# The state's matmuls of a chunked attention on all four 64x64 parts of TensorE: later 64 tokens with the heads of a pair swapped, three copies of y

## The chip, the core and the metric

The kernel runs on one core of one Trainium2 chip. The metric is device microseconds for one execution of the whole program; lower is better. Three runs of the kernel before took 645.78 us in the median (644.98 to 647.78).

## The reference, cut to what matters

The program computes a linear attention with a decaying state and, on its output, two feed-forward layers. For each of 4 batch rows and 8 heads, over 768 tokens of 48 features:

```
for t in range(S):
    cur = einsum('bhd,bhe->bhde', u[None] * kt, vt)
    y[:, :, t] = einsum('bhd,bhde->bhe', rt, state + cur)
    state = wt[..., None] * state + einsum('bhd,bhe->bhde', kt, vt)
x = y.transpose(0, 2, 1, 3).reshape(B * S, H * D)     # 3072 tokens x 384
x = max(x @ w1, x @ w2, x @ w3) @ w_out               # 384 -> 768 -> 384
h = x @ w_in                                          # 384 -> 1024
solu = h * softmax(h)                                 # then a layer norm with g_ln, then @ w_out
```

Everything is float32. The large matrix products are done as three products of rounded high and low parts, so that a product of one 128-wide tile is nine matmuls where its depth is 384.

## The kernel before, in words

The 768 tokens are cut into 6 chunks of 128, and a **unit** u is one chunk of one batch row: 24 units, u // 4 is the chunk. A unit's tokens are taken in two halves of 64 (j = 0, 1), and its 8 heads in 4 pairs p of two heads e = 0, 1. A head has 64 rows (48 and padding), so a pair fills the 128 partitions: head e stands on partitions 64e to 64e + 63. All attention matmuls are 64x64 with 64 columns: what they load comes from one half of the partitions, which picks the array's upper or lower 64 rows, and what they write goes to one half of the partitions of PSUM, which picks its left or right 64 columns. So an instruction uses one of four parts of the array, and each float32 instruction appears in the trace as two matmul records.

A unit's chain, by function and line: prefix and suffix products of the decays on VectorE (`s_sfx` L399, `s_pfx` L416), r scaled by them (`s_rp` L420), scores on TensorE (`s_score` L474), a masked copy of the scores over a diagonal (`s_mask` L481), y within the half (`s_intra` L536, rows by token half j, columns by head e), the state's increments (`s_state2` L582), the state at the middle and at the end (`s_mid` L604, `s_end` L610 on VectorE), and then the state's part of y (`s_inter` L548), which adds to the same PSUM tile as `s_intra`. There y's half j lies in bank j, and head e on partitions 64e of both banks. `s_inter` loads the state of head e from partitions 64e and writes to partitions 64e: two of the four parts. ScalarE then copies y out of PSUM (`s_yT` L662), small DMAs move rows (L668), and `s_xt` (L688, L687) splits it into high and low parts, which are the input of the first feed-forward layer.

The feed-forward layers take tiles of 2 or 3 units (units 0-1, 2-3, 4-5, 6-8, 9-11 and so on): 18 groups of nine matmuls in the first (`stage_a`, L737), then the second (`stage_b`, L767). Each group's result leaves PSUM by ScalarE (L742) or VectorE (L744), then is split (L747, L750). While units 7 to 12 run, a later layer's weights are also converted (`middle_weights`, L318 and L323 on VectorE). After the last unit the last weights are converted and the third and fourth products run, 24 times (L1175, L1252).

The order of all instructions up to there is made by a planner in the file (`Plan`): every task has an engine, an estimated duration in ns, a due time and what it reads and writes. The planner runs them through a model of the engines, and each engine then executes its instructions strictly in the order that comes out. So a changed estimate moves instructions on every engine. y has one PSUM tile of two banks, which the copy of one unit frees for the next.

Of the kernel before, what the change touches and what calls it, by code (L numbers as in the profile page):

```python
# [10 lines left out]
AF = mybir.ActivationFunctionType  # L11
# [3 lines left out]
B, H, T, D = 4, 8, 768, 48  # L15
L = 128
HL = L // 2
NC_ = T // L
NU = B * NC_
NP = H // 2  # L20
# [7 lines left out]
DV = 64  # L28
# [13 lines left out]
BOTH, STEP, AHEAD = 41000, 45600, 20000  # L42
C_DUE = (20000, 2200)
SLACK = 1500
CUT = 0.5
GRP = [(0, 0), (0, 0), (0, 0), (1, 1), (1, 1, 1, 2)]
CW = 384
# [37 lines left out]
class Plan:  # L85
# [8 lines left out]
    def add(self, eng, ns, due, fn, reads=(), writes=(), after=(), take=None, give=None, kb=0, port=0, slack=0):  # L94


        t = Task(len(self.tasks), eng, ns, due, fn)
        t.take, t.give, t.load, t.port, t.slack = take, give, kb, port, slack
        for k in reads:
            t.deps.update(self.wrote.get(k, ()))  # L100
        for k in writes:
            t.deps.update(self.wrote.get(k, ()))
            t.deps.update(self.read.get(k, ()))
        t.deps.update(x for x in after if x is not None)
        for k in reads:
            self.read.setdefault(k, []).append(t)
        for k in writes:
            self.wrote[k], self.read[k] = [t], []
        t.deps.discard(t)
        self.tasks.append(t)  # L110
        return t
# [66 lines left out]
def emit(tc, general, flag, fm, tm, ub, wa, win, wo2, g, cst, half_cst, lmask, out):  # L178
    nc = tc.nc
    PS = bass.MemoryType.PSUM  # L180
    V, A, G, PE = nc.vector, nc.scalar, nc.gpsimd, nc.tensor
# [6 lines left out]
    with ExitStack() as top:  # L188
# [25 lines left out]
        def parts(u):  # L214
            p3 = lambda x: x.rearrange("p (a b) -> p a b", a=NP)
            return p3(r_t[u]), p3(kw_t[u][:, 0:NP * L]), kw_t[u][:, NP * L:]
# [33 lines left out]
        def load_v(u, eng=A):  # L250
            if u < NU and u not in v_t:
                v_t[u] = apool.tile([128, H * DV], F32, tag="v", name=f"v{u}")
                eng.dma_start(v_t[u], tm[u][:, 2 * DM:])
# [203 lines left out]
        def pair(tag, name):  # L457

            t = ps_a.tile([128, 2, 512], F32, tag=tag, name=name)
            return t[:, :, 0:NP * HL].rearrange("p j (a b) -> p j a b", a=NP)  # L460
# [22 lines left out]
        def gen_score(u):  # L483
# [39 lines left out]
            V.memset(d1, 0.0)  # L523
            V.memset(d1[:, :, 0:1], 1.0)

        def s_intra(u):
            d = at[u]
            c = u // B
            v = v_t[u]
            d["yp"] = y = pair("y", f"y{u}")  # L530
            for p in range(NP):
                for j in range(2):
                    for e in range(2):
                        h = 2 * p + e
                        o = slice(64 * j, 64 * j + 64)
                        PE.matmul(y[64 * e:64 * e + 64, j, p], v[o, h * DV:(h + 1) * DV], d["a"][o, h],  # L536
                                  start=(p == 0), stop=(c == 0 and j == 0 and p == NP - 1))

        def s_inter(u):

            d = at[u]
            rt = parts(u)[0]
            for j in (1, 0) if u // B else (1,):
                s = d["st1"] if j else d["st"]
                for p in range(NP):
                    for e in range(2):
                        o = slice(64 * e, 64 * e + 64)
                        PE.matmul(d["yp"][o, j, p], s[o, p], rt[o, p, j * HL:(j + 1) * HL],  # L548
                                  start=False, stop=(p == NP - 1))

        def s_y(u):
            d = at[u]
# [103 lines left out]
        def s_yT(u):  # L656
            ps = at[u]["yp"]
            xf[u] = x = apool.tile([128, NP, L], F32, tag="xf", bufs=1 if general else 3, name=f"xf{u}")
            if general:
                A.activation(x, ps, AF.Copy)  # L660
            else:
                A.activation(x.rearrange("p a (j t) -> p j a t", j=2), ps, AF.Copy)  # L662
            if general:
                s_rows(u)

        def s_rows(u):
            for k in range(KX):
                nc.sync.dma_start(xf[u][3::4, k], xf[u][k::4, KX])  # L668
# [118 lines left out]
        st = {}  # L787
# [65 lines left out]
        def general_phase1():  # L853
# [89 lines left out]
            for j in range(2, n_tile):  # L943
# [9 lines left out]
                if j + 2 == n_tile:  # L953
                    cut = int(len(gs) * CUT)
                    run_groups(gs[:cut], pos, k1, run_items=run_items)
# [11 lines left out]
        def fast_phase1():  # L967
# [6 lines left out]
            def due_of(u):  # L974
                j = tile_of[u]
                last = need[j] - AHEAD
                gap = (need[j] - need[j - 1]) / tiles[j] if j > 1 else START[3]
                return last - gap * (first[j] + tiles[j] - 1 - u)

            def attend(u):  # L980
                d = at.setdefault(u, {})
                D_ = due_of(u)
                late_by = SLACK if u >= first[2] else 0
                late = u // B
                r_, k_, w_ = ("r", u % 2), ("k", u if u < 3 else (u - 3) % 2), ("w", u if u < 3 else (u - 3) % 2)
                rk_ = ("rk", 2 if u == 2 else (u if u < 2 else u - 1) % 2)
                v_, a_, s_, x_ = ("v", u % 2), ("a", u in (1, 3)), ("s", u % 2), ("xf", u % 3)
                sb = ("sbd", u % B)
                add = lambda eng, ns, off, fn, *a, **k: P.add(eng, ns, D_ + off, fn, *a, **k)
                add("SP", 400, -9000, lambda: load_part(u, 2), writes=[w_], kb=260)  # L990
                add("SP", 400, -8000, lambda: load_part(u, 1), writes=[k_], kb=256)
                add("SP", 400, -7000, lambda: load_part(u, 0), writes=[r_], kb=256)
                add("SP", 400, -6500, lambda: load_rk(u, nc.sync), writes=[rk_, "rk in order"], kb=384)
                add("SP", 400, -3000, lambda: load_v(u, nc.sync), writes=[v_, "v in order"], kb=256)
                add("DVE", 1620, 0, lambda: s_sfx(u), [w_], ["sf", "d1", ("pts", u)], port=250)
                add("POOL", 1200, 1500, lambda: d["kt"](), ["sf"], [k_])
                add("DVE", 1230, 2500, lambda: s_pfx(u), [w_, "d1"], ["pf"], port=250)
                add("ACT", 830, 9000, lambda: s_stat(u), [], [w_])
                add("DVE", 680, 3500, lambda: s_rp(u), ["pf"], [r_], port=650)
                add("POOL", 1100, 500, lambda: s_rk(u), [], [rk_])  # L1000
                add("DVE", 1150, 3800, lambda: (s_rku(u), s_diag(u)), [rk_, "u"], [s_], port=600)
                add("POOL", 1050, 4500, lambda: s_dg(u), [s_, "cs"], [a_])
                add("PE", 750, 4600, lambda: s_score(u), [r_, k_], ["sc in order"], slack=late_by, take=("s", ("sc", u)))
                sc = P.tasks[-1]
                if u < NPT:
                    add("PE", 950, 4700, lambda: s_kTp(u), [k_, "ident"], take=("m", ("kTp", u)))
                    add("ACT", 580, 4800, lambda: d["kTe"](), [], ["kT"], after=P.tasks[-1:], give=("m", ("kTp", u)))
                else:
                    add("DVE", 700, 4000, lambda: s_kq(u), [k_], ["sf"])
                    add("SP", 330, 4500, lambda: s_kd(u), ["sf"], [("kd", u % 2)], kb=256)  # L1010
                    add("SP", 2500, 5000, lambda: s_kT(u), [("kd", u % 2)], ["kT"], kb=400)
                add("DVE", 720, 5500, lambda: s_mask(u), ["cs"], [a_], after=[sc], give=("s", ("sc", u)))
                add("PE", 750, 6500, lambda: s_intra(u), [a_, v_], [("y", u), "y in order"], slack=late_by, take=("y", ("y", u)))
                add("PE", 750, 6600, lambda: s_state(u), ["kT", v_], ["ds in order"], P.tasks[-1:], take=("s", ("ds", u)))
                ds = P.tasks[-1]
                if late:
                    add("POOL", 620, 3000, lambda: s_decay(u), [sb, ("pts", u)], ["st"])
                add("DVE" if late else "ACT", 430, 7500, lambda: s_mid(u), ["st"] if late else [], ["st1"], after=[ds],
                    give=None if late < NC_ - 1 else ("s", ("ds", u)))
                if late < NC_ - 1:  # L1020
                    add("DVE", 430, 8000, lambda: s_end(u), ["st1"], [sb], after=[ds], give=("s", ("ds", u)))
                add("PE", 950 if late else 600, 8500, lambda: s_inter(u), ["st", "st1", r_], [("y", u)], slack=late_by)
                add("ACT", 580, 9500, lambda: s_yT(u), [("y", u)], [x_], give=("y", ("y", u)))
                add("SP", 1700, 9800, lambda: s_rows(u), [], [x_], kb=48)

            def split(u, after=()):
# [336 lines left out]
```

## Time and profile before

| what | value |
|---|---|
| median of three runs | 645.78 us |
| the profiled execution | 645.44 us, span of its instructions 643.6 us |
| TensorE busy | 600.4 us (93%) |
| VectorE busy | 429.3 us (67%) |
| ScalarE busy | 295.7 us (46%) |
| GpSimd busy | 382.3 us (59%) |
| mean granted TensorE clock | 0.991 |

PE is TensorE, PEld its weight loads, DVE VectorE, ACT ScalarE, POOL GpSimd, SP the queue that issues the DMAs. The time of an execution is its span and some 2 us around it. A chain of waits follows the work that ended last back to what released each step; its first table gives the shares of the span by line. In a timeline, a row is a start, a duration, the engine, the line, and in brackets the idle time before it and what ended it. Matmuls are pipelined, so their durations overlap: how long a group of them holds the engine is read from one group's start to the next one's.

### The profile page before, as it was taken

How to read it: one execution, taken by the hardware profiler on the slowest of the kernel's cores; microseconds unless marked ns; L12 is line 12 of the kernel's file. 1: busy time of each engine (PE TensorE's matmuls, PEld its weight loads, DVE VectorE, ACT ScalarE, POOL GpSimd, SP SyncE). 2: the span in 40 equal slices, each digit the busy share in tenths (PEclk: the TensorE clock that was granted, in tenths of full speed). 3: DMA queues.
4: the chain of work that ended last, by engine and by line, in shares of the span. 5: the costliest groups of instructions: out<-in, count | busy, mean ns of one | idle time of the engine just before them, and what ended most of it. 6: DMA issues, size and time to landing. Idle time of an engine off the chain costs nothing.

```text
span 643.6 us, 15413 instructions
## 1 busy us (share of the span) xinstructions
PE 600.4 (93%) x5926; PEld 556.6 (86%) x5926; DVE 429.3 (67%) x785; ACT 295.7 (46%) x689; POOL 382.3 (59%) x525
## 2 busy tenths in 40 slices
PE   2577999999999999999999989989999999999996
PEld 2466898999999999999999979987899988888895
DVE  6999977689988755665662222538777777777750
ACT  2878853355453232232232125636555555555552
POOL 4888865567667444454353232655977777777762
PEclk9998999999999999999999999999999999999999
DMA  8968454676564454444332103203776666666661
GB/s 308 345 213 274 150 143 128 177 235 200 165 181 113 130 141 118 130 133 127 104 87 70 21 5 108 78 17 98 146 169 146 148 157 150 152 155 156 155 124 57
DMA packets 174340, 91.93 MB, mean 143 GB/s; under 512 B 140976, under 2 KB 148912, under 8 KB 174256
## 3 DMA queue, kind: packets, MB, share of 16 engines
q1 hardware_dynamic: 174256, 90.84, 52.2%
q8 instruction: 49, 0.80, 0.5%
q14 instruction: 35, 0.29, 0.1%
HBM read 67.87 MB, written 21.76 MB: 139 GB/s over the span
## 4 chain that ended last, share of the span: by engine, by line
PE 73%; DVE 5%; DMA 3%; issue 2%; POOL 2%; ACT 2%; SPq 0%; DVEq 0%; ACTq 0%; POOLq 0%
PE a L737 26%; PE o L1252 16%; PE h L1175 14%; PE b L767 10%; PE y L548 3%; PE sc L474 2%; PE y L536 2%; PE ds L582 1%; DMA fr<-in_fm_dram 1%; DVE x L744 1%; POOL h L750 1%; POOL wo L336 1%; DMA kd<-sf 1%; DVE x L318 1%; DVE sf L399 1%
## 5 line engine op out<-in xcount | busy, mean ns | idle before, releaser
L737 PE MATMUL a<-xh,wah 128*128 128x384 f32 (+1 forms) x432 | 145.8, 337 | 5.2 <-DVE x L744 3.1
L737 PE MATMUL a<-xl,wah 128*128 128x384 f32 (+1 forms) x432 | 140.6, 326 | 0.4 <-POOL xl L687 0.4
L737 PE MATMUL a<-xh,wal 128*128 128x384 f32 (+1 forms) x432 | 140.5, 325 | 0.0
L1252 PE MATMUL o<-wo,lh 128*128 128x384 f32 x368 | 94.0, 337 | 0.0
L737 PEld LDWEIGHTS a<-xh,wah 128*128 128x128 f32 x432 | 83.0, 192 | 9.4 <-DVE x L744 4.4
L1175 PE MATMUL h<-wi,x2h 128*128 128x512 f32 x288 | 90.6, 396 | 0.0
L750 POOL TENSOR_TENSOR h<-x,h 128x384 fp32r<-128x384 f32 (+1 forms) x48 | 51.1, 1065 | 62.3 <-ACT h L747 62.2
L744 DVE TENSOR_TENSOR x<-a,x 128x384 f32<-128x384 f32 (+1 forms) x108 | 54.4, 505 | 46.3 <-PE a L737 35.5
L737 PEld LDWEIGHTS a<-xl,wah 128*128 128x128 f32 x432 | 83.1, 192 | 0.7 <-POOL xl L687 0.7
L737 PEld LDWEIGHTS a<-xh,wal 128*128 128x128 f32 x432 | 83.1, 192 | 0.0
L1244 POOL TENSOR_TENSOR ll<-c,lh 128x512 fp32r<-128x512 f32 x44 | 64.6, 1490 | 21.6 <-ACT lh L1243 21.5
L767 PE MATMUL b<-h,wbh 128*128 128x384 f32 (+1 forms) x288 | 70.9, 332 | 0.0
L1252 PEld LDWEIGHTS o<-wo,lh 128*128 128x128 f32 x368 | 66.8, 188 | 1.8
L1175 PEld LDWEIGHTS h<-wi,x2h 128*128 128x128 f32 x288 | 53.9, 188 | 10.8
L1252 PE MATMUL o<-wo,ll 128*128 128x384 f32 x184 | 62.1, 337 | 0.0
L1175 PE MATMUL h<-wi,x2l 128*128 128x512 f32 x144 | 57.2, 397 | 2.8 <-POOL x2l L798 2.8
L1191 ACT ACTIVATE e<-h,sm 128x512 f32<-128x512 f32 x48 | 32.6, 684 | 56.2 <-DVE sm L1186 56.2
L747 ACT ACTIVATE h<-x 128x384 fp32r<-128x384 f32 (+1 forms) x48 | 23.7, 493 | 67.5 <-DVE x L744 54.3
L767 PEld LDWEIGHTS b<-h,wbh 128*128 128x128 f32 x288 | 50.3, 192 | 1.4
L767 PE MATMUL b<-h,wbl 128*128 128x384 f32 (+1 forms) x144 | 46.8, 325 | 0.0
L1192 DVE SCALAR_TENSOR_TENSOR p<-h,e 128x512 f32<-128x512 f32 x48 | 32.7, 692 | 20.5 <-ACT e L1191 20.5
L429 POOL TENSOR_TENSOR rk<-rk 128x384 f32<-128x384 f32 x23 | 25.1, 1093 | 31.7 <-DMA rk<-in_tm_dram 29.8
(139 smaller groups left out, 1234.6 us busy)
## 6 DMA issues: line engine op xcount, KB each, us to landing
pd<-q SPq DMA_DIRECT2D x23, 512.0 KB, 3.1
c<-pd SPq DMA_DIRECT2D x92, 128.0 KB, 3.7
x<-in_wa_dram SPq DMA_DIRECT2D x24, 384.0 KB, 4.1
rk<-in_tm_dram SPq DMA_DIRECT2D x23, 384.0 KB, 4.4
fr<-in_fm_dram SPq DMA_DIRECT2D x24, 256.0 KB, 4.2
v<-in_tm_dram SPq DMA_DIRECT2D x24, 256.0 KB, 3.5
fk<-in_fm_dram SPq DMA_DIRECT2D x23, 260.0 KB, 3.2
fk<-in_fm_dram SPq DMA_DIRECT2D x23, 256.0 KB, 3.1
```

The source lines that it names most:

```text
L429: G.tensor_tensor(t[:, 0:DM], t[:, 0:DM], t[:, DM:], op=ALU.mult)
L548: PE.matmul(d["yp"][o, j, p], s[o, p], rt[o, p, j * HL:(j + 1) * HL], start=False, stop=(p == NP - 1))
L737: PE.matmul(ps, w_[:, f, m, k], x_[:, k], start=(i == 0), stop=(i == 8))
L744: V.tensor_tensor(t, ps, t, op=ALU.max)
L747: A.activation(hh[:, f], t, AF.Copy)
L750: G.tensor_tensor(hl[:, f], t, hh[:, f].bitcast(F32), op=ALU.subtract)
L767: PE.matmul(ps, w_[:, f, m * 128:(m + 1) * 128], h_[:, f], start=(f == 0 and i == 0), stop=(f == KF1 - 1 and i == 2))
L1175: PE.matmul(ps, x_[:, k], w_[:, k, b * 512:(b + 1) * 512], start=(n_ == 0), stop=(n_ == 8))
L1191: A.activation(e[:, sl], d["h"][b], AF.Exp, bias=col(0), accum_out=col(2 + b))
L1192: V.scalar_tensor_tensor(p[:, sl], d["h"][b], 1.0, e[:, sl], op0=ALU.mult, op1=ALU.mult, accum_out=col(4 + b))
L1244: G.tensor_tensor(ll[:, b], c[:, b], lh[:, b].bitcast(F32), op=ALU.subtract)
L1252: PE.matmul(ps, l_[:, k], w_[:, k], start=(n_ == 0), stop=(n_ == 3 * KF2 - 1))
```

## The change

From unit 6 on (`FOUR = 6`), the second 64 tokens of y have the two heads of a pair on swapped halves of the PSUM partitions: `y_at(u, j, e)` gives partitions 64 * (e ^ j). The state's matmuls of the first half still use the upper left and lower right parts of the array, those of the second half now the two others, and the loop takes both halves of a pair in turn rather than all of one half after the other. `s_intra` writes to the same places. The copy of y from PSUM, one ScalarE instruction of 128x512, becomes three: the first half as it is (128x256), and the second half head by head (64x256 each), which puts the heads back in their places. The planner's estimates change with it: from unit 6 on the state's matmuls count 600 ns rather than 950, the copy 1150 ns rather than 580.

```
+        def y_at(u, j, e):
+            o = 64 * (e ^ j if u >= FOUR else e)
+            return slice(o, o + 64)
...
-                        PE.matmul(y[64 * e:64 * e + 64, j, p], v[o, h * DV:(h + 1) * DV], d["a"][o, h],
+                        PE.matmul(y[y_at(u, j, e), j, p], v[o, h * DV:(h + 1) * DV], d["a"][o, h],
...
-            for j in (1, 0) if u // B else (1,):
+            js = (1, 0) if u // B else (1,)
+            for j, p in [(j, p) for p in range(NP) for j in js] if u >= FOUR else [(j, p) for j in js for p in range(NP)]:
                 s = d["st1"] if j else d["st"]
-                for p in range(NP):
-                    for e in range(2):
-                        o = slice(64 * e, 64 * e + 64)
-                        PE.matmul(d["yp"][o, j, p], s[o, p], rt[o, p, j * HL:(j + 1) * HL],
-                                  start=False, stop=(p == NP - 1))
+                for e in range(2):
+                    o = slice(64 * e, 64 * e + 64)
+                    PE.matmul(d["yp"][y_at(u, j, e), j, p], s[o, p], rt[o, p, j * HL:(j + 1) * HL],
+                              start=False, stop=(p == NP - 1))
...
-                A.activation(x.rearrange("p a (j t) -> p j a t", j=2), ps, AF.Copy)
+                xj = x.rearrange("p a (j t) -> p j a t", j=2)
+                if u < FOUR:
+                    A.activation(xj, ps, AF.Copy)
+                else:
+                    A.activation(xj[:, 0], ps[:, 0], AF.Copy)
+                    for e in range(2):
+                        A.activation(xj[64 * e:64 * e + 64, 1], ps[y_at(u, 1, e), 1], AF.Copy)
...
-                add("PE", 950 if late else 600, 8500, lambda: s_inter(u), ["st", "st1", r_], [("y", u)], slack=late_by)
-                add("ACT", 580, 9500, lambda: s_yT(u), [("y", u)], [x_], give=("y", ("y", u)))
+                add("PE", 600 if u >= FOUR or not late else 950, 8500, lambda: s_inter(u), ["st", "st1", r_], [("y", u)], slack=late_by)
+                add("ACT", 1150 if u >= FOUR else 580, 9500, lambda: s_yT(u), [("y", u)], [x_], give=("y", ("y", u)))
```

TensorE at unit 6, before: the state's part of y (y_1527; st_6 is the state at the middle, the other st the one at the start) between groups of the second layer (b).

```order
L767 MATMUL b_1_1594<-wi,wbh 128x256 x2
L767 MATMUL b_1_1594<-wi,wbl 128x256
L548 MATMUL y_1527<-fr_93,st_6_1589 64x64 x8
L548 MATMUL y_1527<-fr_93,st_1490 64x64 x8
L767 MATMUL b_2_1635<-wi,wbh 128x256 x2
```

The same place now; the lines behind the edits have higher numbers.

```order
L780 MATMUL b_1_1594<-wi,wbh 128x256 x2
L780 MATMUL b_1_1594<-wi,wbl 128x256
L555 MATMUL y_1527<-fr_93,st_6_1589 64x64 x2
L555 MATMUL y_1527<-fr_93,st_1490 64x64 x2
L555 MATMUL y_1527<-fr_93,st_6_1589 64x64 x2
```

The place in the queue is the same; the sixteen matmuls now go by pairs of heads, the second half and then the first, four times.

TensorE at unit 16, before: y within the half (y_3708) and the state's increments (ds_3727) among the groups of the first layer (a_1_2 is the third group of its second 128 columns).

```order
L737 MATMUL a_1_2_3696<-xh_375,wah 128x384
L737 MATMUL a_1_2_3696<-xl_376,wah 128x384
L737 MATMUL a_1_2_3696<-xh_375,wal 128x384
L536 MATMUL y_3708<-a_3539,v_3367 64x64 x16
L582 MATMUL ds_3727<-v_3367,kT_3561 64x64 x16
L737 MATMUL a_2_0_3749<-xh_375,wah 128x384
```

The same place now.

```order
L750 MATMUL a_1_1_3703<-xh_375,wah 128x384
L750 MATMUL a_1_1_3703<-xl_376,wah 128x384
L750 MATMUL a_1_1_3703<-xh_375,wal 128x384
L543 MATMUL y_3715<-a_3557,v_3383 64x64 x16
L589 MATMUL ds_3735<-v_3383,kT_3579 64x64 x16
L750 MATMUL a_1_2_3754<-xh_375,wah 128x384
```

Both stand one group of nine matmuls earlier, and the state's part of y behind them as well. The same is so at units 13, 19 and 20; at unit 10 the state's part alone stands one group earlier, and at units 7 and 8 some stand one group later. Elsewhere TensorE's order is unchanged.

VectorE at unit 16, before: the masked copy of the scores (COPY_PREDICATED) that unit 16's y waits for, and what stands before it (pf is the prefix product of the next unit, x the results of layer groups).

```order
L420 TENSOR_TENSOR fr_95<-fr_95,pf_3482 128x512
L744 TENSOR_TENSOR x_66<-a_0_1_3625,x_66 128x384
L416 SCALAR_TENSOR_TENSOR pf_3666<-fk_97,d_103 128x520
L744 TENSOR_TENSOR x_66<-a_0_2_3638,x_66 128x384
L481 COPY_PREDICATED a_3539<-cs,sc_3649 128x2x4x64
L744 TENSOR_TENSOR x_66<-a_1_1_3682,x_66 128x384
```

The same place now.

```order
L421 TENSOR_TENSOR fr_95<-fr_95,pf_3516 128x512
L757 TENSOR_TENSOR x_66<-a_0_1_3645,x_66 128x384
L757 TENSOR_TENSOR x_66<-a_0_2_3657,x_66 128x384
L482 COPY_PREDICATED a_3557<-cs,sc_3668 128x2x4x64
L417 SCALAR_TENSOR_TENSOR pf_3700<-fk_97,d_103 128x520
L757 TENSOR_TENSOR x_66<-a_1_1_3703,x_66 128x384
```

The scan L416 has moved behind the masked copy, at units 19 and 20 as well; at unit 13 the scan L399 has moved behind it too. Of the conversion steps (a pair of L318 and L323) one fewer than before stands ahead of unit 12's state at the middle (L604).

## Rows read from the trace of the kernel before

**Rows 1.** The page's busy times, and TensorE's busy tenths in 40 slices.
```profile
PE 600.4 (93%) x5926; PEld 556.6 (86%) x5926; DVE 429.3 (67%) x785; ACT 295.7 (46%) x689; POOL 382.3 (59%) x525
...
PE   2577999999999999999999989989999999999996
```

**Rows 2.** The chain that ended last: shares of the span by line.
```profile
PE a L737 26%; PE o L1252 16%; PE h L1175 14%; PE b L767 10%; PE y L548 3%; PE sc L474 2%; PE y L536 2%; PE ds L582 1%; DMA fr<-in_fm_dram 1%; DVE x L744 1%; POOL h L750 1%; POOL wo L336 1%; DMA kd<-sf 1%; DVE x L318 1%; DVE sf L399 1%
```

**Rows 3.** Waits of PE, 114 to 400 us: total, times, longest.
```profile
PE flp L1135 <- DVE fl L810: 2.8, 1, 2.8
PE y L548 <- DVE st L604: 0.2, 1, 0.2
```

**Rows 4.** Timeline of PE around unit 8: start, duration, count at the end.
```profile
130.68 0.69 PE L474 MATMUL sc<-fr,fk 64*64 64x64 f32 x32
131.30 0.39 PE L737 MATMUL a<-xh,wah 128*128 128x256 f32 x1
...
134.73 0.69 PE L536 MATMUL y<-a,v 64*64 64x64 f32 x32
135.25 0.65 PE L582 MATMUL ds<-v,kT 64*64 64x64 f32 x32
135.82 0.39 PE L737 MATMUL a<-xh,wah 128*128 128x256 f32 x1
...
139.25 1.15 PE L548 MATMUL y<-fr,st 64*64 64x64 f32 x32
140.33 0.39 PE L737 MATMUL a<-xh,wah 128*128 128x256 f32 x1
```

**Rows 5.** Windows, L548 alone: stretch, length, PE busy (records).
```profile
114.50:116.00 1.50, 1.15 (x32) 1.01 (x32) 1.00 0.73 139
116.00:376.50 260.50, 19.52 (x544) 17.19 (x544) 1.00 0.47 130
```

**Rows 6.** Groups of ACT by shape: busy us, mean ns, idle before.
```profile
L662 ACT ACTIVATE xf<-y 128x512 f32<-128x512 f32 x24 | 14.2, 593 | 36.7 <-PE y L548 36.5
L742 ACT ACTIVATE x<-a 128x256 f32<-128x256 f32 x18 | 6.8, 378 | 7.5 <-POOL wi L750 5.8 <-PE a L737 0.9 <-POOL h L750 0.7
```

**Rows 7.** Windows, ACT alone.
```profile
118.00:202.00 84.00, 41.84 (x118) 1.00 0.64 184
```

**Rows 8.** Timeline, tile of units 9 to 11: last split, first layer matmul on it.
```profile
196.25 2.21 POOL L687 TENSOR_TENSOR xl<-xf,xh 128x384 fp32r<-128x384 f32 x2
...
202.58 0.33 PE L737 MATMUL a<-xh,wah 128*128 128x384 f32 x1
```

**Rows 9.** Timeline of DVE and PE up to unit 12's state.
```profile
178.64 0.69 DVE L420 TENSOR_TENSOR fr<-fr,pf 128x512 f32<-128x512 f32 x1 [1.85 <-DMA fr<-in_fm_dram]
...
199.86 0.41 DVE L604 TENSOR_TENSOR st<-ds,st 128x256 f32<-128x256 f32 x1
200.33 1.15 PE L548 MATMUL y<-fr,st 64*64 64x64 f32 x32 [0.17 <-DVE st L604]
```

**Rows 10.** Windows, DVE alone.
```profile
118.00:178.60 60.60, 51.82 (x92) 1.00 0.67 199
178.60:202.00 23.40, 22.57 (x34) 1.00 0.54 147
```

**Rows 11.** Timeline around unit 16: the masked copy and the y that needs it.
```profile
258.06 0.73 DVE L481 COPY_PREDICATED a<-cs,sc 128x512 f32<-128x512 int32 x1
260.56 0.70 PE L536 MATMUL y<-a,v 64*64 64x64 f32 x32
```

**Rows 12.** The chain in order of time: start, length, what.
```profile
261.73 3.33 PE a L737 x18
...
285.99 5.41 PE b L767 x30
...
374.74 1.08 PE y L548 x32
...
383.65 10.88 PE b L767 x54
```

More of the change, by code (lines that the diff above doesn't have):

```diff
@@ L44 @@
 SLACK = 1500
+FOUR = 6
 CUT = 0.5
```

## The prediction

> **What bounds the kernel now.** I read the busy times first. TensorE is busy 93% of the span, no other engine over 67%, and its tenths stand at nine from the fifth of 40 slices (about 64 us) on, but for two eights and the last [rows 1]. Busy time alone proves little for a pipelined engine, so the chain of waits comes next: its large lines are all TensorE's, the layers' matmuls (L737, L767, L1175, L1252) and behind them the attention's, of which L548, the line that the change is about, holds 3% of the span, more than L474 or L536 with 2% each [rows 2]. The third view decides: TensorE's own waits from 114 to 400 us, the whole stretch in which units 6 to 23 run. There are two, 0.2 us at unit 12's L548 and 2.8 us at L1135 behind the last unit [rows 3]. In this stretch TensorE's queue has no gaps, so what is taken out of it moves everything behind it forward, and any new wait is a pure loss.
>
> **What the state's matmuls cost, and what is removed.** Around unit 8 I read each block from its first matmul to the first of the next block [rows 4]. The scores, 32 records that go round all four parts of the array, hold TensorE from 130.68 to 131.30: 0.62 us. y within the half and the state's increments, also on four parts, take 134.73 to 135.82, 1.09 us for two blocks, 0.545 each. The state's part of y, as many records of the same shape on two parts, takes 139.25 to 140.33: 1.08 us. After the change this block goes round four parts, in the order upper right, lower left, upper left, lower right: as with the scores, neighbours read from different halves of the partitions and all four parts come round once a pair. I therefore price it at the scores' 0.62 us, which saves 0.46 us.
>
> It occurs in 18 units: 32 records in unit 6 and 544 / 32 = 17 units behind it [rows 5]. 18 x 0.46 = 8.3 us. The bounds: with the 0.545 us of a block inside a pair it would be 18 x 0.535 = 9.6 us; with no gain from four parts, nothing. A loss I exclude: no four-part block in these rows is slower than the two-part one.
>
> **What is added.** ScalarE's copy of y, 593 ns, becomes three. The first has 256 columns, for which the nearest row is the copy of a layer's result out of PSUM with 378 ns [rows 6]. For 64 partitions with 256 columns there is no row; between nothing and the 378 ns of twice the partitions I take 370, as the count of columns is the same. So 3 x 370 = 1110 ns, 0.52 us more for a unit, 9.4 us in all. ScalarE has the room: it is busy 41.84 of the 84 us of its denser stretch [rows 7]. Behind the copy, in its queue, wait copies of layer results and the weight conversion; behind its data, the row DMAs, the split, and the first layer of the unit's tile. I take the tile of units 9 to 11 for the cover: the last low part ends at 196.25 + 2.21 = 198.46, the first matmul on it starts at 202.58 [rows 8]. 4.1 us hide 0.52, so the edit costs nothing; without cover it would be 0.52 for each of six tiles, 3.1 us. The next unit's y takes the PSUM tile only after scores and layer groups of its own.
>
> **What moves.** The planner's new estimates reorder every engine. On TensorE it is little: at four units (13, 16, 19, 20) the y block, the increments and the state's part stand one group of nine matmuls earlier, at unit 10 only the last, at 7 and 8 some one later. One group is 3.33 / 2 = 1.67 us [rows 12]. At unit 16 the masked copy ends at 258.06 + 0.73 = 258.79 and the y that waits for it starts at 260.56 [rows 11]: 1.8 us of room, 0.1 after the move. But the 1.2 us scan ahead of the copy has gone behind it, which gives room back, as at the three others. SP's queue and GpSimd's are reordered in the same way: loads, row moves and splits change places with neighbours, and one may land earlier or later for it. A load that lands late shows as idle time of VectorE, as the 1.85 us at 178.64 [rows 9]; I set these moves at nothing, and their bounds at such a wait gained or lost, which the 1.0 us below takes in.
>
> The weak place is unit 12. VectorE is nearly full there, 22.57 of 23.4 us from 178.6 on, where before it had 51.82 of 60.6 [rows 10]. Its state at the middle ends at 200.27, and TensorE already waits 0.17 us for it [rows 9]. By then TensorE has saved at six units (6 to 11), 6 x 0.46 = 2.8 us, and VectorE has to follow. It can in part: its full stretch starts when a load of r lands, with 1.85 us idle before it [rows 9], and one conversion step that stood ahead of unit 12's state now stands behind. Between 0 and 2.8 us of new waits, I take 1.0, nearer to none since the planner knows both engines' loads.
>
> **The sum.** Of the profiled execution: 645.44 - 8.3 + 1.0 = 638.1 us. Its time is 0.34 us under the median of the three runs, so the forecast is 638.5 us. Behind unit 23 everything starts from TensorE's last attention matmuls, so the whole shift reaches the end.
>
> **Rivals.**
>
> *The early half of the gain is lost.* VectorE doesn't follow before unit 13, and what units 6 to 12 save, 7 x 0.46 = 3.2 us, is waited away at unit 12. Units 13 to 23 keep 11 x 0.46 = 5.1 us: 645.44 - 5.1 + 0.34 = 640.7 us. For it speaks VectorE's full stretch and the 0.17 us wait; against it the 8.8 us that VectorE had free from 118 to 178.6 [rows 10].
>
> *Four parts bring nothing.* What lets a load run beside a matmul would be the half of the partitions it reads from, and the block before already alternates these at every instruction. Then the block stays at 1.08 us and the time at 645.8 us. Against it stand the same rows: the scores alternate in the same way and take 0.62 us, so the half of the columns counts as well [rows 4]. The same time would come if waits ate the gain everywhere. A rule of the Trainium skill is the reason to list this: TensorE: Matmul & The Clock Gate, section Part 3: Packing small matmuls — row/col tiling, has weight loads overlap with matmuls in flight only where the row group differs. By that rule the change saves nothing; the trace's 0.62 against 1.08 us disagrees with it here.
>
> *Slower: the masked copy comes late.* TensorE's queue is strict, and at units 13, 16, 19 and 20 the y block stands 1.67 us nearer to the copy it waits for. If the copy is late at all four, each costs its wait and perhaps the clock: behind the 2.8 us wait at L1135 [rows 3] the next 54 matmuls took 10.88 us, where 30 of the same shape take 5.41, so 54 take 9.74 [rows 12]. That is 2.8 + 1.1 = 3.9 us a time, 15.6 in four, and 645.44 - 8.3 + 15.6 + 0.34 = 653.1 us. It turns slower from 2.9 us at each of the four, which is 11.5 in all: the saving and 0.5%. Against it: the scan that left its place ahead of the copy.
>
> **How the numbers follow.** About 0.5%, 3.2 us, is what a measurement of this kernel can tell from no change. The forecast has 0.64, the early half lost 0.18, no gain 0.10, late copies 0.08. The forecast's own range goes from 636.0 (9.6 us saved, no wait) to 641. Range for eight in ten: 636.0 to 644.5, which takes in the first rival with some ScalarE cover lost (640.7 + 3.1), and leaves out the last two. Faster by over 0.5% (under 642.6): nearly all of the forecast and most of the first rival, 0.77. Same: the rest of these and the third case, 0.15. Slower: 0.08.
>
> **What would show it.** In the profile of the changed kernel, the state's block from its start to the next group should take 0.62 us, not 1.08, in units 6 to 23, and TensorE should reach unit 23's block at about 367 to 368 us rather than 374.7 [rows 12]. The three copies should sum to 1.1 us with no new wait of the first layer for a split. TensorE's waits between 114 and 380 us should stay under 1.5 us, and stand at unit 12 if anywhere. The prediction is wrong if the block stays above 0.8 us; if TensorE waits at the y block for the masked copy, or at several units for VectorE, by more than 4 us together; or if the shift at unit 23 doesn't reach the end.

## The result, and the profile after

The changed kernel takes 637.13 us in the median of four runs (635.76 to 638.16), the kernel before 646.49 us in the four beside it; the ratio is 0.9855, with a 95% interval of 0.9824 to 0.9886. The forecast was 638.5 us, with 636.0 to 644.5. The profiled execution took 638.16 us with a span of 636.4 us, 7.2 us under that of before.

The page's busy times, as in [rows 1], and below them the chain's shares by line, as in [rows 2]:

```profile
PE 594.2 (93%) x5926; PEld 550.2 (86%) x5926; DVE 429.8 (68%) x785; ACT 304.1 (48%) x725; POOL 384.6 (60%) x525
...
PE a L750 28%; PE o L1265 16%; PE h L1188 14%; PE b L780 11%; PE y L555 2%; PE y L543 2%; PE sc L475 2%; PE ds L589 1%; DMA fr<-in_fm_dram 1%; POOL h L763 1%; POOL wo L337 1%; DVE x L757 1%; DMA ct<-in_wo_dram 0%; ACT h L760 0%; ACT e L1204 0%
```

TensorE's busy time fell by 6.2 us with the same number of records, ScalarE's rose by 8.4 us. The state's part of y (now L555) has gone from 3% of the chain to 2%, level with the scores. TensorE's share of busy time is 93% as before: its work and the span shrank together.

TensorE's timeline around unit 8, which answers to [rows 4]: a start, a duration, and the record count at the end of the row. A block's length is the distance from its start to the next row's.

```profile
130.65 0.69 PE L475 MATMUL sc<-fr,fk 64*64 64x64 f32 x32
131.27 0.39 PE L750 MATMUL a<-xh,wah 128*128 128x256 f32 x1
...
135.78 0.69 PE L543 MATMUL y<-a,v 64*64 64x64 f32 x32
136.29 0.65 PE L589 MATMUL ds<-v,kT 64*64 64x64 f32 x32
136.87 0.39 PE L750 MATMUL a<-xh,wah 128*128 128x256 f32 x1
...
140.30 0.69 PE L555 MATMUL y<-fr,st 64*64 64x64 f32 x32
140.93 0.39 PE L750 MATMUL a<-xh,wah 128*128 128x256 f32 x1
```

140.30 to 140.93 is 0.63 us where before it was 1.08; the scores (130.65 to 131.27) and the pair of blocks at 135.78 (1.09 us) are as they were. The windows of the line alone show that this holds for all 18 units, as in [rows 5] (stretch, length, busy time and records of PE, then of PEld): 32 and 544 records again, at 11.81 us rather than 19.52.

```profile
115.40:117.00 1.60, 0.69 (x32) 0.56 (x32) 1.00 0.65 149
117.00:370.00 253.00, 11.81 (x544) 9.48 (x544) 1.00 0.48 134
```

Now the balance. Here is the chain's row (start, length, what) for the first of these blocks before; that of the last stands in [rows 12]:

```profile
114.73 1.08 PE y L548 x32
```

After, the first and the last:

```profile
115.61 0.62 PE y L555 x32
...
368.31 0.62 PE y L555 x32
```

From the first block's start to the last block's end it was 375.82 - 114.73 = 261.09 us and is 368.93 - 115.61 = 253.32 us, 7.77 less. The blocks alone give 18 x 0.46 = 8.28 or, with the 18 lengths of each timeline added up, 19.37 - 11.24 = 8.13. What is missing is TensorE's one new wait, in the list of its waits from 112 to 395 us (total, times, longest), against the 0.2 us of [rows 3]; in the timelines they are 0.59 and 0.17, and 8.13 - 0.42 is 7.71:

```profile
PE flp L1148 <- DVE fl L823: 2.8, 1, 2.8
PE y L555 <- DVE st L611: 0.6, 1, 0.6
```

Of the 7.77 us, 0.88 were lost ahead of unit 6 (its block starts at 115.61 rather than 114.73), where the two kernels have the same instructions in the same order on every engine and only the execution differs. Behind the last block to the end of the span there were 643.6 - 375.82 = 267.8 us and are 636.4 - 368.93 = 267.5. So the shift at the last block's end, 6.9 us, is but for 0.3 us the shift of the end, 7.2.

### The profile page after: what moved, and what is told of

Read it like the earlier page. It is cut to its first block, busy times and chain, and to the rows that moved or that the text cites. A ratio compares the mean times of both kernels' runs of the same rounds, so it can differ in the third digit from the quotient of the medians.

```text
span 636.4 us, 15442 instructions
## 1 busy us (share of the span) xinstructions
PE 594.2 (93%) x5926; PEld 550.2 (86%) x5926; DVE 429.8 (68%) x785; ACT 304.1 (48%) x725; POOL 384.6 (60%) x525
## 4 chain that ended last, share of the span: by engine, by line
PE 76%; DVE 4%; POOL 3%; ACT 2%; DMA 1%; issue 1%; SPq 0%; DVEq 0%; ACTq 0%; POOLq 0%
PE a L750 28%; PE o L1265 16%; PE h L1188 14%; PE b L780 11%; PE y L555 2%; PE y L543 2%; PE sc L475 2%; PE ds L589 1%; DMA fr<-in_fm_dram 1%; POOL h L763 1%; POOL wo L337 1%; DVE x L757 1%; DMA ct<-in_wo_dram 0%; ACT h L760 0%; ACT e L1204 0%
## 5 line engine op out<-in xcount | busy, mean ns | idle before, releaser
L430 POOL TENSOR_TENSOR rk<-rk 128x384 f32<-128x384 f32 x23 | 27.1, 1178 | 36.9 <-DMA rk<-in_tm_dram 36.8
```

What stands on the lines that cost most here:

```text
L430: G.tensor_tensor(t[:, 0:DM], t[:, 0:DM], t[:, DM:], op=ALU.mult)
```

## The experiments

**The changed kernel again (control).** No edit.

> The changed kernel again, unaltered, as the measure for the three others of this group on the same chip. Every theory expects the ratio to the kernel before at 0.983 to 0.989, the state's block of units 6 to 23 at 0.62 us, and one small wait of TensorE for the state at the middle (0.6 us at unit 18 in the first profile).

637.18 us in the median, ratio 0.9857 (0.981 to 0.9904) to a before of 645.96 us. The block took 0.62 us. There was one small wait, 0.36 us, but at unit 12, not at unit 18: its place changes from one execution to the next.

**Two parts, all else as changed (two_parts).**

```
-            o = 64 * (e ^ j if u >= FOUR else e)
+            o = 64 * e
```

> The changed kernel, but y's later half keeps its heads in place, so the state's matmuls use two parts of the array again; the loop over halves and pairs, the three copies and the whole order stay. Theory one (the gain is the two further parts): the block goes back to 1.08 us in 18 units, 18 x 0.46 = 8.3 us, so the ratio to the kernel before is 0.998 to 1.002. Theory two (the gain is the new order, or the loop that alternates the halves): the block or the rest keeps its gain, and the ratio stays at 0.985 to 0.990.

644.7 us, ratio 0.9984 (0.9955 to 1.0014). The gain is gone. In the timeline of unit 8's block:

```profile
139.77 1.15 PE L555 MATMUL y<-fr,st 64*64 64x64 f32 x32
140.85 0.39 PE L750 MATMUL a<-xh,wah 128*128 128x256 f32 x1
```

1.08 us again, and the timeline has 1.07 or 1.08 for every unit from 6 to 23. This kernel has the new order (the same on every engine as the changed kernel's), the loop that alternates the halves, and the three copies; together these bring no time that the runs can tell. Theory one holds, and theory two falls. The two further parts are worth 7.5 us between its median and the control's; from unit 6's block to the end of unit 23's it is 260.90 us here and 253.12 in the control, 7.8 us.

The trace also shows what the new order does by itself, with TensorE as slow as before. Unit 12's state at the middle, and the block that needs it:

```profile
197.64 0.41 DVE L611 TENSOR_TENSOR st<-ds,st 128x256 f32<-128x256 f32 x1
...
199.53 1.15 PE L555 MATMUL y<-fr,st 64*64 64x64 f32 x32
```

VectorE starts this state 2.2 us earlier than before (199.86 in [rows 9]), of which some 0.6 us is the earlier start of unit 6 in this execution; the rest is the order's, since TensorE had saved nothing yet.

**Four parts in the order of before (old_order).**

```
-                add("PE", 600 if u >= FOUR or not late else 950, 8500, lambda: s_inter(u), ["st", "st1", r_], [("y", u)], slack=late_by)
-                add("ACT", 1150 if u >= FOUR else 580, 9500, lambda: s_yT(u), [("y", u)], [x_], give=("y", ("y", u)))
+                add("PE", 950 if late else 600, 8500, lambda: s_inter(u), ["st", "st1", r_], [("y", u)], slack=late_by)
+                add("ACT", 580, 9500, lambda: s_yT(u), [("y", u)], [x_], give=("y", ("y", u)))
```

> The changed kernel, but the planner's estimates are those of the kernel before (950 and 580 ns), so every engine has the order of before, with four parts and three copies. Theory one (four parts alone, order of no account): block 0.62 us, the ratio as the control's within 0.002. Theory two (the new estimates were needed): new waits, above all at unit 12 where VectorE was full, 2 to 3 us in all, so a ratio of 0.990 to 0.993.

639.6 us, ratio 0.9893 (0.9857 to 0.9928), between the two expectations; its interval overlaps the control's, so the times alone don't part them. The trace does. TensorE's waits in this kernel:

```profile
PE y L555 <- DVE st L611: 3.3, 3, 1.6
PE flp L1148 <- DVE fl L823: 2.8, 1, 2.8
```

They stand at units 11, 12 and 15 (1.62, 0.86 and 0.82 us), where the control waits 0.36 us in all. Here is the one at unit 12, VectorE's state at the middle and TensorE's block that needs it (idle time before it in brackets):

```profile
199.56 0.41 DVE L611 TENSOR_TENSOR st<-ds,st 128x256 f32<-128x256 f32 x1
...
200.03 0.69 PE L555 MATMUL y<-fr,st 64*64 64x64 f32 x32 [0.86 <-DVE st L611]
```

With the old estimates VectorE is behind the earlier TensorE: 3.3 - 0.4 = 2.9 us, about the 2.4 us between the medians. So the new estimates were worth something, which theory two said, though less than half of what the parts bring.

Where VectorE loses the time ahead of units 11 and 12 can be read: at the scaled r (L421) that opens its full stretch. First this kernel, then the control:

```profile
177.93 0.91 DVE L421 TENSOR_TENSOR fr<-fr,pf 128x512 f32<-128x512 f32 x1 [1.38 <-DMA fr<-in_fm_dram]
...
176.67 0.67 DVE L421 TENSOR_TENSOR fr<-fr,pf 128x512 f32<-128x512 f32 x1
```

The load of r is issued at 171.83 us here, behind a load of weights, and at 170.65 in the control, ahead of it; so it was 171.78 in the kernel before and 170.32 in the changed kernel. With the old order VectorE waits for it, 1.38 us here and 1.85 before [rows 9]; with the new one it doesn't. The wait at unit 15 has another source: there VectorE had sat idle for 2.95 us until GpSimd's L403 was done.

**One copy of y (one_copy).**

```
-                    A.activation(xj[:, 0], ps[:, 0], AF.Copy)
-                    for e in range(2):
-                        A.activation(xj[64 * e:64 * e + 64, 1], ps[y_at(u, 1, e), 1], AF.Copy)
+                    A.activation(xj, ps, AF.Copy)
```

> The changed kernel with one copy of y from unit 6 on in place of three; it leaves the heads of the later 64 tokens swapped, which changes what is computed and no other duration. ScalarE does 9.4 us less work. Theory one (the copies are hidden): the ratio as the control's within 0.002, and ScalarE's busy time 9 to 10 us lower. Theory two (the copies delay rows or layer results that TensorE waits for): up to 3 us faster than the control.

638.16 us, ratio 0.9885 (0.9846 to 0.9924). The busy times of its page:

```profile
PE 590.3 (93%) x5926; PEld 546.8 (86%) x5926; DVE 429.4 (68%) x785; ACT 295.2 (47%) x689; POOL 384.7 (61%) x525
```

ScalarE is busy 9.3 us less than in the control (304.5), and the kernel is not faster; its ratio is inside the control's interval. The times alone would leave room for a microsecond or two of theory two, the traces don't: from unit 6's block to the end of unit 23's it is 252.68 us here and 253.12 in the control, of which 0.36 is the control's one wait. Theory one: the two further copies are hidden.

**Six orders of the same sixteen matmuls (six_orders).**

```
+                seq = [
+                    [(j, p, e) for p in P_ for j in js for e in E_],
+                    [(j, p, e) for j in js for p in P_ for e in E_],
+                    [(c ^ e, p, e) for c in E_ for p in P_ for e in E_],
+                    [(j, p, e) for e in E_ for p in P_ for j in js],
+                    [(j, p, e) for j in js for e in E_ for p in P_],
+                    [(j, p, e) for p in P_ for e in E_ for j in js],
+                ][u % 6]
```

> The changed kernel with the state's sixteen matmuls of a unit in one of six orders, by unit modulo six, three units each; sums and places are the same. Modulo 0: as changed, four parts. 1: the later half wholly before the earlier, two parts at a time on a diagonal. 2: two parts at a time in one half of the columns, so that neighbours differ in the half of the rows. 3: two parts at a time in one half of the rows, neighbours differ in the half of the columns. 4: one part at a time. 5: four parts, two neighbours from one half of the rows. Theory one (a part is free again after its own load and matmul, whatever the others do; 32 records in 0.92 us on two parts and 0.46 on four, with 0.16 at the ends): 0.62, 1.08, 1.08, 1.08, 2.0 and 0.62 us. Theory two (only the half of the rows counts): orders 0, 1 and 2 alike, 3 and 4 alike and slower. Theory three (only the half of the columns counts): orders 3 fast, 2 slow as 4.

The chain from unit 6 to unit 11, one order each:

```profile
115.25 0.62 PE y L566 x32
128.47 0.91 PE y L566 x30
140.29 0.91 PE y L566 x30
154.77 0.91 PE y L566 x30
168.96 1.47 PE y L566 x32
183.69 0.62 PE y L566 x32
```

The chain counts 30 of a block's 32 records in three of the rows; in the timeline, from the block's first record to the next row, these are 0.90 or 0.91 as well. Units 12 to 23 repeat these numbers. The one execution took 643.23 us; the blocks come to 16.3 us there and to 11.2 in the changed kernel. Four parts take 0.62 us whichever half neighbours share; two parts take 0.91 whether they differ in the rows, in the columns or in both; one at a time takes 1.47. Theories two and three fall, since neither half of the array counts by itself. Theory one has the ranking right and two sizes wrong: 1.08 was expected for two parts and 2.0 for one. The difference from the kernel before, whose block uses the same two parts to its end, is that here the pair of parts changes once in the middle, and in the one-part order the part changes three times. One figure, 0.17 us given back at each change, fits both: 1.08 - 0.17 = 0.91, and 2.0 - 3 x 0.17 = 1.49.

**Two instructions in a row on a part (runs_of_two).**

```
+                seq = [
+                    [(j, p, e) for h in E_ for j in js for e in E_ for p in (2 * h, 2 * h + 1)],
+                    [(j, p, e) for j in js for h in E_ for e in E_ for p in (2 * h, 2 * h + 1)],
+                    [(j, p, e) for p in P_ for j in js for e in E_],
+                ][u % 3]
```

> The changed kernel with the state's sixteen matmuls of a unit in one of three orders, by unit modulo three, six units each; sums and places are the same. Modulo 0: four parts in turn, but two instructions in a row on a part. 1: the later half before the earlier, so two parts at a time, two instructions in a row on each. 2: as changed. Theory one, worked out from the 0.62, 0.91 and 1.47 us of the six orders (a part takes 57.5 ns for a record, and three records of one part can be under way or waiting before the queue stands still): 0.79, 1.02 and 0.62 us. Theory two (it only counts how many parts a unit's block uses): 0.62 us for modulo 0, 0.91 for modulo 1. Theory three (neighbours on one part undo the overlap): both at 1.4 us or more.

The timeline of units 6 to 8, each block and the row behind it:

```profile
113.61 0.76 PE L563 MATMUL y<-fr,st 64*64 64x64 f32 x32
114.29 0.50 PE L788 MATMUL b<-wi,wbh 128*128 128x256 f32 x2
...
126.88 1.03 PE L563 MATMUL y<-fr,st 64*64 64x64 f32 x32
127.84 0.39 PE L758 MATMUL a<-xh,wah 128*128 128x256 f32 x1
...
138.75 0.69 PE L563 MATMUL y<-fr,st 64*64 64x64 f32 x32
139.38 0.39 PE L758 MATMUL a<-xh,wah 128*128 128x256 f32 x1
```

0.68, 0.96 and 0.63 us; the one execution took 638.48 us. No theory has the first two numbers. Two in a row on a part cost 0.06 and 0.05 us over the same parts taken in turn, far from undoing the overlap, so theory three falls; theory one's 0.79 and 1.02 are too much and theory two's 0.62 and 0.91 too little. How many records of one part can be ahead stays open.

**The swap from unit 4 on (from_unit_4).**

```
-FOUR = 6
+FOUR = 4
```

> The changed kernel with the swap from unit 4 on, so that all units with a state at their start have it. Theory one (every block that TensorE is the bound of gains 0.46 us): units 4 and 5 add 0.9 us at most, the ratio to the kernel before 0.982 to 0.988. Theory two (units 4 and 5 run where TensorE waits for others, and the new order brings waits there): no gain or a loss, a ratio of 0.986 to 0.995.

639.58 us, ratio 0.9922 (0.99 to 0.9945) to a before of 644.57 us on another chip. There is no further gain. The new order, which differs ahead of unit 6 too, brings waits; this is the largest, at unit 12 again:

```profile
199.34 0.41 DVE L611 TENSOR_TENSOR st<-ds,st 128x256 f32<-128x256 f32 x1
...
199.80 0.69 PE L555 MATMUL y<-fr,st 64*64 64x64 f32 x32 [1.69 <-DVE st L611]
```

With another 0.4 us at unit 7's y, for which the profile names no releaser, that is 2.1 us, more than the 0.9 us that units 4 and 5 could have given. Theory two. Whether it is slower than the changed kernel the ratios don't settle: the interval is clear of the changed kernel's first one (up to 0.9886) and touches the control's (up to 0.9904), and the chips differ. No version better than the changed kernel came out of these runs.

**The traces added up.** From the start of unit 6's block to the end of unit 23's every trace can be split into the 18 blocks, TensorE's waits, and all else that it does there.

| trace | stretch, us | blocks | waits | all else |
|---|---|---|---|---|
| before | 261.09 | 19.37 | 0.17 | 241.55 |
| changed | 253.32 | 11.24 | 0.59 | 241.49 |
| control | 253.12 | 11.23 | 0.36 | 241.53 |
| two_parts | 260.90 | 19.35 | 0 | 241.55 |
| old_order | 256.24 | 11.22 | 3.30 | 241.72 |
| one_copy | 252.68 | 11.25 | 0 | 241.43 |
| six_orders | 257.85 | 16.32 | 0 | 241.53 |
| runs_of_two | 255.12 | 13.63 | 0 | 241.49 |

The last column stays within 0.3 us. So in this stretch the blocks and the waits are the whole difference between the kernels; the copies, the loop and the moves act on it, if at all, through waits. from_unit_4 is left out, since it has other work in this stretch.

## Why the prediction was right

- **TensorE without gaps from unit 6 on.** Right. What left its queue came off the end almost whole: 8.13 us of blocks, 7.77 us from the first block to the last, and 267.5 us behind it where there were 267.8. Unit 23's block starts at 368.3, just past the forecast 367 to 368, because unit 6's starts 0.88 us later in this execution.
- **0.62 us for the block, from the scores.** Right to 0.01 us at every unit. The upper bound of 9.6 us, from a block beside another block, didn't come about: the state's block stands alone between layer groups, as the scores do.
- **Two parts as the cause.** Right, by two_parts: with two parts the whole gain goes. The rival that four parts bring nothing is refuted. The rule of the Trainium skill that stood beside it (TensorE: Matmul & The Clock Gate, section Part 3: Packing small matmuls — row/col tiling), that weight loads overlap with matmuls in flight only where the row group differs, would have left the time as it was; the blocks' 8.1 us disagree. By six_orders the half of the rows is of no account by itself: two parts in one half of the rows take 0.91 us, two parts in different halves as well.
- **Three copies at no cost.** Right. By shape, as in [rows 6]:

```profile
L673 ACT ACTIVATE xf<-y 128x256 f32<-128x256 f32 x18 | 6.8, 378 | 34.4 <-PE y L555 34.4
L675 ACT ACTIVATE xf<-y 64x256 f32<-64x256 f32 x36 | 13.7, 379 | 0.4
```

  378 + 2 x 379 = 1136 ns against the 1110 assumed. The 64-partition copies, for which there was no row, take as long as those with 128. TensorE's list of waits, shown above, has none of the first layer for a split. The cover at the tile of units 9 to 11 shrank but holds: its last low part ends at 195.71 + 2.23 = 197.94, the first matmul on it starts at 200.02, 2.1 us where [rows 8] gave 4.1.

```profile
195.71 2.23 POOL L700 TENSOR_TENSOR xl<-xf,xh 128x384 fp32r<-128x384 f32 x2
...
200.02 0.33 PE L750 MATMUL a<-xh,wah 128*128 128x384 f32 x1
```

- **1.0 us of new waits, at unit 12.** This term was too large, and its place was not sure: 0.36 us at unit 12 in the control, and 0.59 us at unit 18 in the profiled execution. The one at unit 18 is not the wait that was feared: VectorE was not full there, but sat idle for 3.93 us until GpSimd's L403 was done, and the state stands behind that in its queue.

```profile
289.99 0.71 DVE L639 STREAM_TRANSPOSE sf<-fk 128x512 f32<-128x512 f32 x1 [3.93 <-POOL fk L403]
...
291.06 0.69 PE L555 MATMUL y<-fr,st 64*64 64x64 f32 x32 [0.59 <-DVE st L611]
```

  At unit 12 VectorE followed, as these rows show against [rows 9]: its state is ready at 197.39, TensorE comes at 198.24.

```profile
196.98 0.41 DVE L611 TENSOR_TENSOR st<-ds,st 128x256 f32<-128x256 f32 x1
...
198.24 0.69 PE L555 MATMUL y<-fr,st 64*64 64x64 f32 x32
```

  The windows of VectorE, beside [rows 10], show it in sums: it does more ahead of the full stretch, 54.17 us rather than 51.82, and has 21.35 to do in it rather than 22.57.

```profile
118.00:178.60 60.60, 54.17 (x93) 1.00 0.69 201
178.60:202.00 23.40, 21.35 (x34) 1.00 0.60 157
```

  The fear itself was sound: with the old estimates (old_order) and with the swap from unit 4 (from_unit_4) unit 12 is among the places where TensorE waits, and the sum is 3.3 and 2.1 us. "The planner knows both engines' loads" was the reason given for the small value, and old_order with two_parts is its test. What the new order moved was more than the conversion step that the prediction named: the load of r, whose move it set at nothing within bounds, is issued 1.5 us earlier, and the 1.85 us that VectorE had waited for it are gone.
- **The masked copy in time at unit 16.** Right. It ends at 253.45 + 0.73 = 254.18 and y starts at 255.09, 0.9 us of room after the move, where 0.1 and what the moved scan gives back had been counted.

```profile
253.45 0.73 DVE L482 COPY_PREDICATED a<-cs,sc 128x512 f32<-128x512 int32 x1
...
255.09 0.69 PE L543 MATMUL y<-a,v 64*64 64x64 f32 x32
```

What the single terms don't say is the spread: eight runs of the changed kernel and its control lie between 634.73 and 639.18 us, and 0.88 us of the difference of the two profiles came from ahead of the change; over all traces but from_unit_4's, whose order up to there is the same, unit 6's block starts between 113.6 and 115.5 us. One profile against another is no better than that. The medians differ by 9.4 us where the profiles differ by 7.3 and the terms give 7.7; that the median came so near to the forecast is in part the luck of the draw. A slip in the prediction is of no account: with 9.6 us saved its sum gives 636.2, not the 636.0 at which its range begins.

## What to carry to other kernels

Where an engine's queue shows no waits over a whole stretch, count what the edit takes out of it by the distance from one block's start to the next block's, price the new form by a block of the same shape that stands alone in the same way, and the sum comes out at the end. For 64x64 matmuls let neighbouring instructions go round all four parts of the array; a placement that puts both halves of a result on the same partitions leaves two of them idle. And when an engine in a planned order gets faster, tell the planner: the engine behind it has to be early too, and so have the loads that this one waits for.

## What the runs showed of the hardware

Two things were not expected. A ScalarE copy out of PSUM of 64 partitions takes as long as one of 128 (379 and 378 ns for 256 columns). And a sequence on few parts of the array is not as slow as its count of parts says, if the parts change on the way: 32 records take 1.08 us on the same two parts throughout, 0.91 when the pair changes once, 1.47 one part at a time with three changes, 0.68 on four parts with two instructions in a row on each, and 0.62 on four in turn. A change could give time back if records for a free part start ahead of records that still wait for theirs, and the trace of the kernel before has such starts. At unit 5 the scores, on four parts, stand right behind a block on two:

```profile
105.35 1.08 PE L548 MATMUL y<-fr,st 64*64 64x64 f32 x29
106.22 0.27 PE L474 MATMUL sc<-fr,fk 64*64 64x64 f32 x1
106.22 0.22 PE L548 MATMUL y<-fr,st 64*64 64x64 f32 x1
106.22 0.27 PE L474 MATMUL sc<-fr,fk 64*64 64x64 f32 x1
106.27 0.23 PE L548 MATMUL y<-fr,st 64*64 64x64 f32 x2
```

The first two records of the scores start among the last three of y. The difference of the blocks on two and on four parts, 0.46 us for eight records more on a part, makes some 58 ns for a record on its part (an estimate), so the 0.17 us given back at a change is the time of three records. But theory one of runs_of_two was worked out with three records, and its sizes didn't come out; how far records can be ahead stays open.
